# Loading V by whole heads (32 KB rows) in a one-token attention kernel that is bound by its loads

## The chip, the cores and the metric

The kernel runs on one core of one Trainium2 chip; no other core is used by it. The metric is the device time of one execution in microseconds (us). The kernel before takes 325.06 us, the median of four runs (324.63 to 325.5).

Engine names: PE is the matrix engine, DVE the vector engine, ACT the scalar engine, SP the engine whose sequencer issues the loads. "P·V" is the product of the softmax weights with V.

## The reference

```python
B, H, Sq, Sk, D = 1, 16, 1, 8192, 256      # q: one token; k and v: 64 MB each, bfloat16
def reference(q, k, v):
    scale = q.shape[-1] ** -0.5
    scores = jnp.einsum("bhqd,bhkd->bhqk", q, k) * scale
    p = _softmax(scores, axis=-1)
    return jnp.einsum("bhqk,bhkd->bhqd", p, v)
```

Every byte of K and V is read once, 134.2 MB in all. There are 16 heads, with 4 MB of K and 4 MB of V each.

## The kernel before

A head's K or V lies in SBUF (the core's on-chip memory) as 128 partitions by 64 columns of 256 numbers: partition p holds 64 neighbouring rows, 32 KB. The kernel loads *halves*: 32 of the 64 columns, 128 rows of 16 KB, 2 MB. There are four half-head buffers for K and four for V. Loads are issued by SP in one fixed order. A load into a buffer waits until that buffer's last reader is done, and holds up all loads behind it.

```python
LAST_CUT = (16, 8, 4, 4)      # columns per DMA: second half of V of the last head
BEFORE_CUT = (16, 16)         # first half of V of the last head
LAG = 4                       # V runs four halves (two heads) behind K
...
for n, kx in enumerate(kseq):             # kseq: (head, half) in order
    items.append(("k", *kx))
    while nv <= n - LAG:
        items.append(("v", *kseq[nv])); nv += 1
items += [("v", *kx) for kx in kseq[nv:]]
...
        if n >= slots:                    # the buffer's last readers
            waits = [f"{kind}free{n - slots}"] + ([f"ktfree{n - slots}"] if kind == "k" else [])
```

The scores of 24 of the 32 columns of each half are made by DVE (multiply and add up along the row, one instruction per column). The other 8 columns go to PE, which transposes them (`k_turn`) and multiplies (`k_score`). PE also makes P·V, one matmul of 256 output columns for each column of V. PE's program for head h, in order:

```python
softmax(h - 1)                 # transposes the maxima of head h-1
k_turn(2 * h)                  # first half of K of head h
softmax2(h - 1); k_score(2 * h); lmm(h - 1)
pv(2 * (h - 2))                # P·V, first half of head h-2
k_turn(2 * h + 1); k_score(2 * h + 1)
pv(2 * (h - 2) + 1)            # P·V, second half of head h-2
final(h - 2)
```

(`softmax`, `softmax2` and `lmm` are the small matmuls of the softmax: the maximum, its broadcast and the sum. `final` hands the finished head to ACT.) After the last head PE runs P·V of heads 14 and 15 with the small matmuls of the last softmax between them. PE takes its instructions strictly in this order, and each P·V matmul waits for the DMA that brings its column.

## Time and profile before

| | before |
|---|---|
| time, median | 325.06 us |
| span of the profiled execution | 322.9 us |
| first load packet starts, last load lands | 1.7 us, 319.6 us |
| V of head 13 fully landed | 299.9 us |
| last P·V matmul ends | 320.9 us |
| DVE busy, PE busy | 86%, 69% |

Here is the page of the kernel before, cut to three rows of its slices. The span is cut in 40 slices of 8.07 us. The PEclk row is PE's granted clock in tenths of full speed, the DMA row the busy share of the 16 DMA engines in tenths (9 is 90% or more), and GB/s what they moved.

```profile
PEclk9999999999698998989595989777989697897799
DMA  7999999999999999999999999999999999999993
GB/s 276 421 436 428 421 430 428 424 426 426 431 428 426 428 428 428 432 426 424 432 426 434 426 424 430 428 428 429 426 430 426 430 427 428 428 426 428 426 417 120
```

The DMA engines are full from the second slice to the last but one, at about 428 GB/s. This is a stream of loads, and everything else has to keep it full and to end soon after it. The Trainium skill ("DMA: Bandwidth & Descriptors", "Where 436 GB/s comes from") gives a ceiling of 435 GB/s for the SBUF ports. The trace agrees: it stands 1.6% below it. The same section says that for loads from HBM a lower figure binds, about 358 GB/s; that does not hold in this trace, where one core loads alone.

The end is the only part that is not stream. Here is PE's timeline of the kernel before at the end (start, length, engine, line, operation and number of instructions; in brackets the idle time before and what ended it):

```profile
299.91 8.81 PE L607 MATMUL acc<-Vb,E 128*1 128x256 bf16 x64 [1.33 <-DMA Vb<-in_v_dram]
308.56 0.38 PE L547 MATMUL misc<-ident,m 128*1 128x128 f32 x2
309.74 1.91 PE L607 MATMUL acc<-Vb,E 128*1 128x256 bf16 x16 [0.80 <-DMA Vb<-in_v_dram]
...
313.69 7.17 PE L607 MATMUL acc<-Vb,E 128*1 128x256 bf16 x64
```

At 299.91 us PE begins with the second half of V13, which has just landed; the first half is done already. At 309.74 it waits once more, for V14's second half. From there it has 96 columns left and never waits again: it is behind the stream, and it ends 1.2 us after the last landing.

The trace's load packets (one is one row of one load on one of the 16 engines) have these median times: 84 ns for 2 KB, 159 ns for 4 KB, 312 ns for 8 KB, 614 ns for 16 KB. So each costs about 75.5 ns per 2 KB and about 10 ns besides.

### The profile page before, as it was taken

The page shows a single profiled execution, that of the slowest core. Times are in us where ns is not written, and L with a number is a line of the kernel's source. Part 1 is how long each engine was busy: PE and PEld are TensorE (multiplying, and loading weights), DVE is VectorE, ACT ScalarE, POOL GpSimd, SP SyncE. Part 2 cuts the span into 40 slices and gives each one's busy share as a digit, 9 for nine tenths or more (in the row PEclk, how much of TensorE's full clock was granted, in tenths as well). Part 3 has the DMA queues.
Part 4 walks back from the last instruction along what each step waited for, and adds up shares of the span by engine and source line. Part 5 has one row for each costly group of instructions (what it writes and reads, how often), then busy time and mean ns, then how long its engine had stood idle before and what let it go on. Part 6 is the DMA issues. An engine that isn't in the chain of part 4 may idle for free.

```text
span 322.9 us, 6455 instructions
## 1 busy us (share of the span) xinstructions
PE 222.2 (69%) x2166; PEld 155.6 (48%) x2166; DVE 277.8 (86%) x1607; ACT 94.1 (29%) x185; POOL 0.2 (0%) x4
## 2 busy tenths in 40 slices
PE   1554328766586858686987756886665966668897
PEld 0333225655364635454564534564543644455565
DVE  3799999999999999999998988889988889888600
ACT  3362321432324242323142242212422123232010
POOL 0000000000000000000000000000000000000000
PEclk9999999999698998989595989777989697897799
DMA  7999999999999999999999999999999999999993
GB/s 276 421 436 428 421 430 428 424 426 426 431 428 426 428 428 428 432 426 424 432 426 434 426 424 430 428 428 429 426 430 426 430 427 428 428 426 428 426 417 120
DMA packets 10271, 134.37 MB, mean 416 GB/s; under 512 B 1154, under 2 KB 1171, under 8 KB 1940
## 3 DMA queue, kind: packets, MB, share of 16 engines
q1 hardware_dynamic: 10224, 134.22, 98.1%
q8 instruction: 5, 0.08, 0.1%
q14 instruction: 6, 0.05, 0.0%
q10 hardware_dynamic: 36, 0.02, 0.0%
HBM read 134.23 MB, written 0.01 MB: 416 GB/s over the span
## 4 chain that ended last, share of the span: by engine, by line
DVE 52%; DMA 37%; PE 5%; issue 5%; DVEq 1%; ACT 0%; SPq 0%
DVE prod L360 48%; DMA Kb<-in_k_dram 19%; DMA Vb<-in_v_dram 18%; PE acc L607 5%; DVE S L360 2%; DVE g L332 1%; DVE colf L286 0%; DVE recip L341 0%; DVEq L145 0%; DVE m L379 0%; ACT o L621 0%; DVEq L138 0%; DVEq L139 0%; SPq L319 0%; PE misc L558 0%
## 5 line engine op out<-in xcount | busy, mean ns | idle before, releaser
L360 DVE CUSTOM_DVE_ANT_0 prod<-Kb,qbc 128x256 bf16<-128x256 bf16 x768 | 269.1, 411 | 24.6 <-DMA Kb<-in_k_dram 15.7
L607 PE MATMUL acc<-Vb,E 128*1 128x256 bf16 x1024 | 147.4, 314 | 8.8 <-DMA Vb<-in_v_dram 8.8
L607 PEld LDWEIGHTS acc<-Vb,E 128*1 128x1 bf16 x1024 | 96.3, 96 | 52.4 <-DMA Vb<-in_v_dram 9.9
L502 ACT ACTIVATE KT<-tp 128x1024 bf16<-128x1024 bf16 x64 | 62.0, 1021 | 118.2 <-PE tp L493 118.2
L360 DVE DVE_READ_ACCUMULATOR2_ANT S<- 128x1 f32 x768 | 56.8, 74 | 0.0
L493 PE MATMUL tp<-identb,Kb 128*128 128x128 bf16 x512 | 38.2, 234 | 7.8 <-DMA Kb<-in_k_dram 7.8
L493 PEld LDWEIGHTS tp<-identb,Kb 128*128 128x128 bf16 x512 | 32.3, 105 | 15.7 <-issue 14.2
L519 PE MATMUL spe<-qcur,KT 128*128 128x1 bf16 x512 | 20.6, 165 | 19.7 <-ACT KT L502 19.7
L558 PE MATMUL misc<-g,ones_row 1*128 1x1 f32 x32 | 7.1, 287 | 36.1 <-DVE g L332 36.1
L519 PEld LDWEIGHTS spe<-qcur,KT 128*128 128x128 bf16 x512 | 16.4, 99 | 24.5 <-ACT KT L502 24.3
L621 ACT ACTIVATE o<-acc,recip 1x256 bf16<-1x256 f32 x16 | 7.4, 464 | 69.4 <-PE acc L607 69.4
L558 PEld LDWEIGHTS misc<-g,ones_row 1*128 1x128 f32 x32 | 5.7, 221 | 39.1 <-DVE g L332 38.8
L547 PE MATMUL misc<-ident,m 128*1 128x128 f32 x34 | 7.1, 293 | 18.6 <-DVE m L379 18.6
L547 PEld LDWEIGHTS misc<-ident,m 128*1 128x1 f32 x34 | 1.9, 82 | 22.0 <-DVE m L379 21.4
L565 ACT ACTIVATE negb<-misc 128x1 f32<-128x1 f32 x16 | 2.7, 171 | 27.4 <-PE misc L558 27.4
L332 DVE TENSOR_REDUCE g<-misc 1x1 f32<-1x128 f32 x17 | 4.7, 274 | 5.2 <-PE misc L547 5.2
L341 DVE RECIPROCAL recip<-misc 1x1 f32<-1x1 f32 x17 | 2.6, 151 | 4.6 <-PE misc L587 4.6
L572 ACT ACTIVATE E<-S,negb 128x64 bf16<-128x64 f32 x16 | 5.6, 348 | 0.7 <-ACT negb L565 0.2
L587 PE MATMUL misc<-ones_col,lsum 128*1 128x1 f32 x34 | 3.2, 164 | 3.7 <-ACT E L572 3.7
L439 ACT ACTIVATE qbc<-qb 128x256 bf16<-128x256 bf16 x14 | 5.6, 400 | 0.0
L532 ACT ACTIVATE S<-spe 128x16 f32<-128x16 f32 x16 | 2.9, 183 | 7.2 <-PE spe L519 7.2
L413 PE MATMUL tp<-q,identb 16*128 16x256 bf16 x15 | 4.1, 406 | 0.6 <-ACT qb L422 0.5
(29 smaller groups left out, 22.7 us busy)
## 6 DMA issues: line engine op xcount, KB each, us to landing
Kb<-in_k_dram SPq DMA_DIRECT2D x31, 2048.0 KB, 24.3
Vb<-in_v_dram SPq DMA_DIRECT2D x30, 2048.0 KB, 29.5
Vb<-in_v_dram SPq DMA_DIRECT2D x3, 1024.0 KB, 16.5
Kb<-in_k_dram SPq DMA_DIRECT2D x1, 1024.0 KB, 8.5
Kb<-in_k_dram SPq DMA_DIRECT2D x2, 256.0 KB, 3.0
Kb<-in_k_dram SPq DMA_DIRECT2D x1, 512.0 KB, 6.5
Vb<-in_v_dram SPq DMA_DIRECT2D x1, 512.0 KB, 12.7
Vb<-in_v_dram SPq DMA_DIRECT2D x2, 256.0 KB, 13.0
```

The source lines that it names most:

```text
L332: lambda e: e.tensor_reduce(g[0:1, s : s + 1], misc[s][0:1, MT0 : MT0 + P], AX.X, ALU.max),
L360: lambda e, slot=slot, c=c, col=col, h=h, r=(ttr - 1) % PROD: e.tensor_tensor_reduce(out=prod[:, r * D : (r + 1) * D], in0=Kb[slot][:, c * ...
L413: lambda e, i=i, src=src: e.matmul(bank[:, i * D : (i + 1) * D], lhsT=src[0], rhs=src[1], start=True, stop=True),
L439: lambda e: e.activation(out=qbc[:, s * D : (s + 1) * D], in_=qb[:, (h - 2) * D : (h - 1) * D], func=ACT.Copy),
L493: lambda e, c=c, hf=hf, i=(b * NH + hf) * P, view=view: e.transpose(view[:, i : i + P], Kb[slot][:, c * D + hf * P : c * D + (hf + 1) * P] ...
L502: lambda e, gn=gn, view=view: e.activation(out=KT[gn % KT_SLOTS][:, :], in_=view[:, 0 : GROUP * D], func=ACT.Copy),
L519: lambda e, b=b, hf=hf, oc=oc, gn=gn: e.matmul(spe[sl(h)][:, oc : oc + 1], lhsT=KT[gn % KT_SLOTS][:, (b * NH + hf) * P : (b * NH + hf + 1) ...
L547: lambda e: e.matmul(misc[s][0:1, MT0 : MT0 + P], lhsT=m[:, s : s + 1], rhs=ident[:, :], start=True, stop=True),
L558: lambda e: e.matmul(misc[s][:, BC0 : BC0 + 1], lhsT=ones_row[0:1, :], rhs=g[0:1, s : s + 1], start=True, stop=True),
L572: lambda e: e.activation(out=E[:, s * J : (s + 1) * J], in_=S[:, s * J : (s + 1) * J], func=ACT.Exp, bias=negb[:, h : h + 1], scale=SCALE, ...
L607: lambda e, c=c, col=col: e.matmul(a[0:1, 0:D], lhsT=E[:, col : col + 1], rhs=Vb[slot][:, c * D : (c + 1) * D], start=(x == 0 and c == 0), ...
L621: lambda e: e.activation(out=o[0:1, h * D : (h + 1) * D], in_=acc[s][0:1, 0:D], func=ACT.Copy, scale=recip[0:1, s : s + 1],),
```

## The change

The intent: a row of V becomes 32 KB instead of 16 KB, so that there are half as many rows with their fixed cost, and the last head's V comes in eight pieces so that PE can follow it closely.

- V has two buffers of a whole head, and heads 0 to 13 come in one 4 MB DMA each. K is still loaded in halves.
- A V buffer is freed by the whole head: the load of V of head h waits for both halves of P·V of head h-2.
- V follows one head behind K up to head 7 and two heads behind from head 8.
- P·V of both halves of head h-2 stands after the scores of head h.
- V14 comes in pieces of 32, 16 and 16 columns, V15 in 16, 8, 8, 8, 8, 8, 4 and 4.

```diff
-K_SLOTS = 2 * UNROLL
-V_SLOTS = 2 * UNROLL
...
-FIRST_CUT = (4, 4, 8, 16)
-LAST_CUT = (16, 8, 4, 4)
-BEFORE_CUT = (16, 16)
-LAG = 4
+K_CUTS = {0: (4, 4, 8, 16, 32)}
+V_CUTS = {14: (32, 16, 16), 15: (16, 8, 8, 8, 8, 8, 4, 4)}
+LAG_FROM = 8
...
+        for h in range(H):
+            loads.append(("k", h))
+            done = sum(kind == "v" for kind, _ in loads)
+            loads += [("v", x) for x in range(done, h + 1 - (1 if h < LAG_FROM else 2))]
+        loads += [("v", x) for x in range(sum(kind == "v" for kind, _ in loads), H)]
+
+        def cuts(kind, h):
+            return K_CUTS.get(h, (HALF, HALF)) if kind == "k" else V_CUTS.get(h, (J,))
...
                 if kind == "k":
...
+                    if h >= 2:
+                        waits = [f"kfree{2 * (h - 2) + i}", f"ktfree{2 * (h - 2) + i}"]
                 else:
...
+                    if h >= 2:
+                        waits = [f"vfree{2 * (h - 2)}", f"vfree{2 * (h - 2) + 1}"]
...
                 if h + 1 < H:
                     q_row(h + 1)
-                if h >= 2:
-                    pv(2 * (h - 2))
...
             if h >= 2:
+                pv(2 * (h - 2))
                 pv(2 * (h - 2) + 1)
                 final(h - 2)
```

More of the change, by code (lines that the diff above doesn't have):

```diff
@@ L178, in sem @@
             return ctx.enter_context(nc.semaphore(name))
-        Kb = [sb([P, HALF * D], dt, "Kb") for _ in range(K_SLOTS)]
-        Vb = [sb([P, HALF * D], dt, "Vb") for _ in range(V_SLOTS)]
+        Kb = [sb([P, J * D], dt, "Kb") for _ in range(2)]
+        Vb = [sb([P, J * D], dt, "Vb") for _ in range(2)]
         KT = [sb([P, GROUP * D], BF16, "KT") for _ in range(KT_SLOTS)]
@@ L213, in bass_standalone__mha_softmax__decode_kernel @@
         sems = {e: sem(f"s_{e}") for e in plan.ops}
-        s_k = [sem(f"s_k{i}") for i in range(K_SLOTS)]
-        s_v = [sem(f"s_v{i}") for i in range(V_SLOTS)]
-        s_first = [sem(f"s_f{i}") for i in range(len(FIRST_CUT) - 1)]
-        s_last = [sem(f"s_l{i}") for i in range(len(LAST_CUT) + len(BEFORE_CUT) - 2)]
+        s_k = [sem(f"s_k{i}") for i in range(4)]
+        s_v = [sem(f"s_v{i}") for i in range(2)]
+        s_piece = {}
         s_q = sem("s_q")
@@ L243, in bass_standalone__mha_softmax__decode_kernel, with pieces @@
         kseq = [(h, x) for h in range(H) for x in range(2)]
-        NIT = 2 * H
-        items, nv = [], 0
-        for n, kx in enumerate(kseq):
-            items.append(("k", *kx))
-            while nv <= n - LAG:
-                items.append(("v", *kseq[nv]))
-                nv += 1
-        items += [("v", *kx) for kx in kseq[nv:]]
-        n_of = {kx: n for n, kx in enumerate(kseq)}
-        def cuts(kind, n):
-            if kind == "k" and n == 0:
-                return FIRST_CUT
-            if kind == "v" and n == NIT - 1:
-                return LAST_CUT
-            if kind == "v" and n == NIT - 2:
-                return BEFORE_CUT
-            return (HALF,)
-        def landed(kind, n, c0, c1):
-            names, at = [], 0
-            if kind == "k" and n and n % K_SLOTS == 0:
-                names = [f"k{n}.0"] + [x for x in landed(kind, 0, c0, c1) if x != "k0.0"]
-                return names
-            for i, w in enumerate(cuts(kind, n)):
-                if at < c1 and at + w > c0:
-                    names.append(f"{kind}{n}.{i}")
-                at += w
-            return names
+        loads = []
+        for h in range(H):
[5 more added lines that the diff above has]
+            return K_CUTS.get(h, (HALF, HALF)) if kind == "k" else V_CUTS.get(h, (J,))
+        def landed(kind, n, c0, c1):
+            h, x = kseq[n]
+            def pieces(h):
+                at = 0
+                for i, w in enumerate(cuts(kind, h)):
+                    if at < x * HALF + c1 and at + w > x * HALF + c0:
+                        yield i
+                    at += w
+            if kind == "k" and h and h % 2 == 0:
+                return [f"k{h}.{x}"] + [f"k0.{i}" for i in pieces(0) if 0 < i < len(cuts(kind, 0)) - 1]
+            return [f"{kind}{h}.{i}" for i in pieces(h)]
         def dve(fn, name=None, waits=(), sem=None):
@@ L301, in bass_standalone__mha_softmax__decode_kernel @@
         plan.op("act", lambda e: e.dma_start(q16[:, :], q[0, :, 0, :]), "q", dma=(s_q, 16))
-        for kind, h, x in items:
-            n = n_of[(h, x)]
-            slots, sem_l, t, buf = (K_SLOTS, s_k, k, Kb) if kind == "k" else (V_SLOTS, s_v, v, Vb)
-            slot = n % slots
-            waits = []
-            if n >= slots:
-                waits = [f"{kind}free{n - slots}"] + ([f"ktfree{n - slots}"] if kind == "k" else [])
-            cs = cuts(kind, n)
+        for kind, h in loads:
+            t, buf = (k, Kb) if kind == "k" else (v, Vb)
+            cs = cuts(kind, h)
             at = 0
             for i, wd in enumerate(cs):
+                waits = []
+                last = i == len(cs) - 1
                 if kind == "k":
-                    s = sem_l[slot] if i == 0 else s_first[i - 1]
-                else:
-                    s = sem_l[slot] if i == len(cs) - 1 else s_last[i + (len(LAST_CUT) - 1) * (n == NIT - 2)]
+                    s = s_k[2 * (h % 2) + (i > 0)] if i == 0 or last else None
+                    if h >= 2:
+                        waits = [f"kfree{2 * (h - 2) + i}", f"ktfree{2 * (h - 2) + i}"]
+                else:
+                    s = s_v[h % 2] if last else None
+                    if h >= 2:
+                        waits = [f"vfree{2 * (h - 2)}", f"vfree{2 * (h - 2) + 1}"]
+                if s is None:
+                    s = s_piece[(kind, h, i)] = sem(f"s_{kind}{h}_{i}")
                 used[id(s)] = used.get(id(s), 0) + 16
@@ L318, in bass_standalone__mha_softmax__decode_kernel @@
                     "sp",
-                    lambda e, b=buf[slot], t=t, h=h, c=x * HALF, at=at, wd=wd: e.dma_start(
-                        b[:, at * D : (at + wd) * D], cols(t, h, c + at, c + at + wd)
+                    lambda e, b=buf[h % 2], t=t, h=h, at=at, wd=wd: e.dma_start(
+                        b[:, at * D : (at + wd) * D], cols(t, h, at, at + wd)
                     ),
-                    f"{kind}{n}.{i}",
+                    f"{kind}{h}.{i}",
                     waits,
@@ L349, in bass_standalone__mha_softmax__decode_kernel @@
         for n, (h, x) in enumerate(kseq):
-            slot = n % K_SLOTS
             if x == 0 and h % UNROLL == 0:
@@ L359, in bass_standalone__mha_softmax__decode_kernel @@
                 dve(
-                    lambda e, slot=slot, c=c, col=col, h=h, r=(ttr - 1) % PROD: e.tensor_tensor_reduce(
+                    lambda e, c=c, x=x, col=col, h=h, r=(ttr - 1) % PROD: e.tensor_tensor_reduce(
                         out=prod[:, r * D : (r + 1) * D],
-                        in0=Kb[slot][:, c * D : (c + 1) * D],
+                        in0=Kb[h % 2][:, (x * HALF + c) * D : (x * HALF + c + 1) * D],
                         in1=qbc[:, sl(h) * D : (sl(h) + 1) * D],
@@ L480, in k_turn @@
             h, x = kseq[n]
-            slot = n % K_SLOTS
             for gi in range(NG):
@@ L494, in k_turn @@
                                 view[:, i : i + P],
-                                Kb[slot][:, c * D + hf * P : c * D + (hf + 1) * P],
+                                Kb[h % 2][:, (x * HALF + c) * D + hf * P : (x * HALF + c) * D + (hf + 1) * P],
                                 identb[:, :],
@@ L600, in pv @@
             h, x = kseq[n]
-            slot = n % V_SLOTS
             a = acc[sl(h)]
@@ L609, in pv @@
                         lhsT=E[:, col : col + 1],
-                        rhs=Vb[slot][:, c * D : (c + 1) * D],
+                        rhs=Vb[h % 2][:, (x * HALF + c) * D : (x * HALF + c + 1) * D],
                         start=(x == 0 and c == 0),
```

## The prediction

> **What bounds it now.** The 16 DMA engines. The page's slices and the stage table give a DMA share of 1.00 and 427 to 428 GB/s from 12 to 300 us; the packets leave no gap between 1.7 us and the last landing at 319.7 us. DVE is busy 86%, PE 69%; landings come 24 to 30 us after the issue, so the queue never runs dry. Only the end is not DMA: the timeline shows PE waiting at 309.7 us for the second half of V14, then running 96 P·V matmuls without a DMA wait to 320.9 us, 1.2 us after the last V piece landed.
>
> **What the change does.**
>
> 1. *Longer packets.* In the trace's packets a 16 KB row takes 614 ns, 8 KB 312, 4 KB 159, 2 KB 84: about 75.5 ns per 2 KB plus 10 ns each. So a 32 KB row should take about 1,218 ns against 2 x 614. 14 heads x 8 rows per engine x 10 ns is -1.1 us; fewer completion writes (9 ns each) -0.1; finer last pieces +0.2. Net -1.1 us, all on the path. The Trainium skill ("DMA: Bandwidth & Descriptors", "Where 436 GB/s comes from") puts the ceiling at 435 GB/s; this trace is at 428, so longer rows of V alone cannot give 1%.
>
> 2. *Coarser landings.* P·V of a head waits for all of V (4 MB, 9.8 us of stream), and PE does both halves in one run. Matmuls in P·V start 109 ns apart at full clock, 213 ns at half. In the steady state this is off the path. I reckon 20 us or more of slack for slots in the late phase, 4 us in the early one; DVE waits about 2 us more per head for the maximum (PE is in P·V), inside its slack (17.3 us busy per 19.6 us head). Tightest is V2: its slot frees after P·V of head 0, near 63 us (begin 53.5, 64 matmuls, some 20 cold); the stream needs it near 64. Expected loss 0.3 us, at worst 2 to 3.
>
> 3. *The tail.* V13 now lands whole, about 20 us before the end, and PE has 192 matmuls left instead of 160 or fewer: 192 x 109 ns = 20.9 us, 0.9 us for the small softmax matmuls, and 1.7 to 3 us of half clock, because PE idles about 7 us before V13 lands. (The Trainium skill, "TensorE: Matmul & The Clock Gate", Part 1, says that an idle window of about 3.4 us brings the half clock; the trace shows such stretches, one at 300.8 us.) So PE ends about 3.9 us after the last landing, against 1.2: +2.7 us. The eight pieces help only a PE that waits; here it lags.
>
> Sum: -1.1 + 0.3 + 2.7 = about +1.6 us: **326.6 us**, 8 in 10 between 323.2 and 329.2. Faster by over 2%: 2%; within 2%: 95%; slower by over 2%: 3%.
>
> **What would show it.** Packets of 32,768 bytes near 1,218 ns; last landing about 1 us earlier (318.6); DMA share still 1.00, save perhaps a small dip near 64 us; P·V of V13, V14 and V15 as one unbroken PE run from about 299 us to 322.5 us, with no wait for the eight pieces; a half-clock stretch at its start; no new DVE-for-K waits.
>
> **What would make it wrong.** A PE that catches up with V15's pieces: then the tail ends 0.6 us after the last landing, the result near 323 us. Long rows split by the hardware: no gain in 1. V2 or V3 issued late: a gap in the stream.

## The result, and the profile after

| | before | after |
|---|---|---|
| time, median (range) | 325.06 us (324.63 to 325.5) | 329.27 us (329.14 to 329.35) |
| ratio | | 1.0129 (1.0111 to 1.0147) |
| span of the profiled execution | 322.9 us | 327.5 us |
| V13 fully landed | 299.9 us | 300.8 us |
| last load landed | 319.6 us | 323.5 us |
| last P·V matmul ends | 320.9 us | 325.4 us |

The change makes the kernel 1.3% slower. A ratio here is the mean time of one kernel's fast runs over the mean of the other's in the same rounds, so it isn't quite the ratio of the medians. The bracket is a 95% interval.

The same three rows of the page, after (slices of 8.19 us):

```profile
PEclk9999999969679695976959795875959578595799
DMA  7999999899999999999999999999999999999694
GB/s 255 430 446 422 419 448 410 316 448 404 438 427 454 404 430 446 416 440 420 424 450 418 426 462 396 436 422 430 436 428 460 397 432 452 404 432 430 278 356 160
```

Two holes have come into the stream: one in the eighth slice (316 GB/s) and one in the third slice from the end (278 GB/s). PE's clock is at half more often. The stage view places the holes. Its columns are the stretch in us, its length, the busy time with the number of instructions of PE, of PE's weight loads, of DVE, ACT and POOL, then PE's clock, the DMA share and GB/s. First the kernel before, in the stretches of the two holes:

```profile
61.80:64.40 2.60, 2.29 (x28) 1.66 (x26) 2.56 (x16) 1.19 (x2) 0.00 (x0) 1.00 1.06 441
64.40:67.00 2.60, 0.86 (x18) 0.76 (x18) 2.60 (x16) 1.63 (x4) 0.00 (x0) 1.00 0.99 422
308.40:312.00 3.60, 2.80 (x25) 1.84 (x23) 0.28 (x1) 0.00 (x1) 0.00 (x0) 1.00 1.02 423
```

The same stretches of the changed kernel:

```profile
61.80:64.40 2.60, 2.38 (x28) 1.57 (x25) 2.57 (x17) 1.09 (x2) 0.00 (x0) 1.00 0.77 233
64.40:67.00 2.60, 0.55 (x12) 0.54 (x13) 2.60 (x16) 1.45 (x3) 0.00 (x0) 1.00 0.71 290
308.40:312.00 3.60, 3.60 (x35) 2.77 (x34) 0.00 (x0) 0.47 (x1) 0.00 (x0) 1.00 0.23 52
```

The share, the second number from the end, falls from about 1 to 0.77 and 0.71 in the early hole, which is 2.6 x 0.23 + 2.6 x 0.29 = 1.4 us of the whole stream, and to 0.23 in the late one, which is 2.8 us. This view counts a packet whole where it starts. With packets cut at the window's edges, the trace has the engines idle for 1.6 us between 60 and 66 us, and for 3.2 us in the late window. The 16 rows that start the stream again after the early hole also took 1.87 us each in the mean, 0.65 us more than the usual 1.22. So the early hole is about 2.3 us of stream in this run.

What the early hole waits for is seen in the loads that SP issues (the timeline of SP's queue, after), with PE's timeline before it:

```profile
53.84 0.37 PE L510 MATMUL spe<-qcur,KT 128*128 128x1 bf16 x8 [0.54 <-ACT KT L493]
54.14 8.71 PE L597 MATMUL acc<-Vb,E 128*1 128x256 bf16 x64
```

```profile
36.30 8.70 SPq L312 DMA_DIRECT2D Kb<-in_k_dram  x2
62.88 0.33 SPq L312 DMA_DIRECT2D Vb<-in_v_dram  x1
63.26 1.45 SPq L312 DMA_DIRECT2D Kb<-in_k_dram  x2
```

V2 needs V0's buffer. P·V of head 0, 64 matmuls, runs from 54.14 to 62.85 us, and V2 is issued at 62.88. K of head 3, the last load ahead of it, was issued by 45.0 us, and its second half completes on the first of the 16 engines at 61.80 us and on the last at 64.88 us. So most engines ran dry. In the kernel before, the same stretch of SP's queue has K of head 4 ahead of V2, and V2's first half, which needs only the first half of V0's buffer, goes out at 56.38 us:

```profile
44.72 0.43 SPq L319 DMA_DIRECT2D Vb<-in_v_dram  x1
53.85 0.33 SPq L319 DMA_DIRECT2D Kb<-in_k_dram  x1
56.38 0.33 SPq L319 DMA_DIRECT2D Vb<-in_v_dram  x1
```

PE's timeline at the end, after:

```profile
296.91 0.37 PE L510 MATMUL spe<-qcur,KT 128*128 128x1 bf16 x8 [0.56 <-ACT KT L493]
300.92 13.37 PE L597 MATMUL acc<-Vb,E 128*1 128x256 bf16 x96 [3.63 <-DMA Vb<-in_v_dram]
314.12 0.38 PE L538 MATMUL misc<-ident,m 128*1 128x128 f32 x2
...
318.29 7.15 PE L597 MATMUL acc<-Vb,E 128*1 128x256 bf16 x64
```

PE now stands idle for 3.6 us until the whole of V13 is there, and has 192 columns left instead of 160. From 300.92 us to 325.43 us, 24.5 us, it waits for no load again: the eight pieces of V15 are there when it comes to them. The first 96 matmuls take 13.37 us. In the trace 25 of the 192 stand 213 ns apart, and nearly all others 109 ns: PE's clock is at half from 296.3 to 306.5 us. In the kernel before, the stretch from V13's landing to PE's end was 320.9 - 299.9 = 21.0 us.

So the change of the span of 4.6 us has two visible parts: PE begins on the V that it waited for 1.0 us later (300.92 against 299.91), and needs 3.6 us more from there (24.5 against 20.9). By the spacing of the matmuls these 3.6 us are 32 more of them at 109 ns (3.5 us) and ten more at half clock (25 against 15 in the kernel before, 1.0 us), less about 1.0 us that the kernel before waits for V14.

The packets: a 32 KB row takes 1,215 ns (median), a 16 KB row 613 ns, so 11 ns are saved per pair of rows.

### The profile page after: what moved, and what is told of

It is laid out like the page before. It is cut to its first block, busy times and chain, and to the rows that moved or that the text cites. A ratio compares the mean times of both kernels' runs of the same rounds, so it can differ in the third digit from the quotient of the medians.

```text
span 327.5 us, 6434 instructions
## 1 busy us (share of the span) xinstructions
PE 225.7 (69%) x2166; PEld 163.0 (50%) x2166; DVE 277.6 (85%) x1607; ACT 93.6 (29%) x185; POOL 0.2 (0%) x4
## 4 chain that ended last, share of the span: by engine, by line
DMA 45%; DVE 24%; PE 23%; issue 4%; ACT 3%; SPq 0%; DVEq 0%
DMA Vb<-in_v_dram 27%; DVE prod L352 22%; PE acc L597 21%; DMA Kb<-in_k_dram 18%; ACT KT L493 2%; PE tp L484 1%; DVE S L352 1%; PE misc L549 1%; DVE g L325 0%; ACT E L563 0%; SPq L312 0%; DVE colf L276 0%; PE spe L510 0%; PE misc L578 0%; ACT negb L556 0%
## 5 line engine op out<-in xcount | busy, mean ns | idle before, releaser
L597 PE MATMUL acc<-Vb,E 128*1 128x256 bf16 x1024 | 142.5, 311 | 19.2 <-DMA Vb<-in_v_dram 19.2
L352 DVE DVE_READ_ACCUMULATOR2_ANT S<- 128x1 f32 x768 | 55.7, 73 | 0.0
L484 PE MATMUL tp<-identb,Kb 128*128 128x128 bf16 x512 | 44.7, 257 | 11.6 <-DMA Kb<-in_k_dram 11.6
L484 PEld LDWEIGHTS tp<-identb,Kb 128*128 128x128 bf16 x512 | 38.2, 117 | 17.0 <-issue 13.1
L510 PE MATMUL spe<-qcur,KT 128*128 128x1 bf16 x512 | 21.8, 167 | 19.8 <-ACT KT L493 19.8
L510 PEld LDWEIGHTS spe<-qcur,KT 128*128 128x128 bf16 x512 | 17.4, 103 | 26.0 <-ACT KT L493 25.9
L549 PE MATMUL misc<-g,ones_row 1*128 1x1 f32 x32 | 7.4, 297 | 24.8 <-DVE g L325 24.8
L414 ACT ACTIVATE qb<-tp 128x512 bf16<-128x512 f32 x7 | 3.9, 595 | 3.3 <-PE tp L405 3.3
```

Source lines behind the costliest of these rows:

```text
L352: lambda e, c=c, x=x, col=col, h=h, r=(ttr - 1) % PROD: e.tensor_tensor_reduce(out=prod[:, r * D : (r + 1) * D], in0=Kb[h % 2][:, (x * HAL ...
L414: lambda e: e.activation(out=qbc[:, a * D : b * D] if first else qb[:, (a - 2) * D : (b - 2) * D], in_=bank[:, 0 : (b - a) * D], func=ACT. ...
L484: lambda e, c=c, hf=hf, i=(b * NH + hf) * P, view=view: e.transpose(view[:, i : i + P], Kb[h % 2][:, (x * HALF + c) * D + hf * P : (x * HA ...
L510: lambda e, b=b, hf=hf, oc=oc, gn=gn: e.matmul(spe[sl(h)][:, oc : oc + 1], lhsT=KT[gn % KT_SLOTS][:, (b * NH + hf) * P : (b * NH + hf + 1) ...
L549: lambda e: e.matmul(misc[s][:, BC0 : BC0 + 1], lhsT=ones_row[0:1, :], rhs=g[0:1, s : s + 1], start=True, stop=True),
L597: lambda e, c=c, col=col: e.matmul(a[0:1, 0:D], lhsT=E[:, col : col + 1], rhs=Vb[h % 2][:, (x * HALF + c) * D : (x * HALF + c + 1) * D], s ...
```

## The experiments

The theory after the result (A): the longer rows give about 1.1 us. The early hole takes that back and more, because V2's buffer comes free by the whole head. At the end PE gets V13 too late and too cold, and the late hole costs nothing, because PE is behind the stream there. Each experiment changes the changed kernel, called "after" below. Each was timed against the kernel before in its own rounds; the median of the kernel before there was 324.92 us for e1 to e4 and 324.88 us for the others. All gave correct results.

### e1: V15 in a buffer of its own

Rival: the hole of 2.8 us at 308 us is what costs. V15 needs V13's buffer, and P·V of head 13 ends at 310.8 us. The K buffer of head 14 is free by then, so V15 goes there and nothing else changes.

```diff
+                    if h == H - 1:
+                        waits = [f"{w}{x}" for x in (2 * H - 4, 2 * H - 3) for w in ("kfree", "ktfree")]
-                    if h >= 2:
+                    elif h >= 2:
                         waits = [f"vfree{2 * (h - 2)}", f"vfree{2 * (h - 2) + 1}"]
...
-                        rhs=Vb[h % 2][:, ...],
+                        rhs=(Kb[0] if h == H - 1 else Vb[h % 2])[:, ...],
```

(The destination of the load is changed likewise, and V15's last piece has a semaphore of its own.)

> V of head 15 goes into K's buffer 0, which is free by then, so that its load no longer waits for P.V of head 13. Theory A (the end is bound by PE: 192 matmuls from the landing of V13 on, without a wait): the stream's gap at 308.4 to 312.0 us disappears, the last landing comes 3 us or more earlier, yet the P.V run still starts near 300.9 us and ends near 325.4 us: time 329.3 us, within 0.4. Rival G (the gap in the stream, 3.2 us of 16 engines, costs time): 326 us.

Measured: 329.36 us (328.63 to 329.58), ratio 1.0129 (1.0112 to 1.0145), the same as after. The hole is gone in the stage view of e1:

```profile
308.40:312.00 3.60, 3.60 (x35) 2.77 (x33) 0.00 (x0) 0.46 (x1) 0.00 (x0) 1.00 1.00 412
```

The last load lands 320.9 us into the span instead of 323.5. Yet the chain that ended last (start, length, what) is after's:

```profile
300.91 0.14 issue
301.04 13.44 PE acc L599 x96
...
318.62 7.02 PE acc L599 x64
```

So a hole of 2.8 us in the stream, 15 us before the end, costs nothing: PE is the limit there. The rival falls.

### e2: V13 in two halves; e8: its control

PE's loop over heads is a rolled loop whose bodies have to wait for the same things, so heads 14 and 15 are taken out of it and written out.

```diff
-V_CUTS = {14: (32, 16, 16), 15: (16, 8, 8, 8, 8, 8, 4, 4)}
+V_CUTS = {13: (32, 32), 14: (32, 16, 16), 15: (16, 8, 8, 8, 8, 8, 4, 4)}
...
-        plan.mark("pe")          # end of PE's loop: now in front of head 14
```

> V of head 13 lands in two halves; the last two heads of PE's loop are unrolled for it (a rolled body may not differ). Theory A: P.V of head 13 starts near 297.3 us instead of 300.9, the slot of V15 frees near 307 us so that the gap at 308 us goes too, and PE ends 3.3 to 4.6 us earlier, bound by PE or by the last landing: time 324.7 to 326.0 us. A theory in which the end is bound by the eight pieces of V15 themselves (small transfers): no gain, 329 us.

> Control: the changed kernel with the last two heads of PE's loop unrolled and nothing else, as e2, e5 and e7 needed it. Theory A and every rival: 329.3 us, within 0.4.

Measured: e8, the unrolling alone, 329.19 us, ratio 1.0126 (1.0111 to 1.0141): no effect. e2: 325.98 us (325.8 to 327.11), ratio 1.0040 (1.0017 to 1.0064), 3.3 us under after. PE's timeline of e2:

```profile
298.20 12.02 PE L597 MATMUL acc<-Vb,E 128*1 128x256 bf16 x96
...
314.21 4.53 PE L597 MATMUL acc<-Vb,E 128*1 128x256 bf16 x40
318.99 1.03 PE L597 MATMUL acc<-Vb,E 128*1 128x256 bf16 x8 [0.25 <-DMA Vb<-in_v_dram]
320.26 1.91 PE L597 MATMUL acc<-Vb,E 128*1 128x256 bf16 x16 [0.23 <-DMA Vb<-in_v_dram]
```

PE begins 2.7 us earlier, right after the scores of head 15 and with no wait, and now does wait for the last pieces of V15, 0.2 us at a time. One of the 14 whole-head DMAs, cut in two, gives back most of the loss. The late hole is gone too, because V13's buffer is freed earlier.

### e7: the clock of PE at V13's landing

How much of the end is the half clock? Forty-two matmuls without use keep PE occupied while it waits for V13. They multiply the identity's first column with a row of q into columns of a PSUM bank that nothing reads.

```diff
             k_turn(2 * h)
+            if h == H - 1:
+                warm(10)
...
             k_turn(2 * h + 1)
+            if h == H - 1:
+                warm(10)
             k_score(2 * h + 1)
+            if h == H - 1:
+                warm(22)
```

> The changed kernel with 42 matmuls without use (into a free part of a PSUM bank) in PE's program for head 15, ahead of P.V of head 13, and the last two heads of PE's loop unrolled for them. Theory A (28 of the 192 matmuls of the final run are at half clock, 3.0 us, because PE was little used before V13 landed): the half-clock stretch from 296 to 306 us shrinks or goes, the run of 24.5 us falls to 21.5 to 22.5 us, time 326.3 to 327.5 us. Rival (the slow matmuls come from V's data just landing, or the end is bound by something else): 329.3 us.

Measured: 326.58 us (326.29 to 327.3), ratio 1.0047 (1.0033 to 1.0062), 2.6 us under its control e8. In e7's timeline the first 96 matmuls of the end take 10.64 us instead of 13.37:

```profile
298.51 2.56 PE L625 MATMUL acc<-qb,identb 128*1 128x256 bf16 x22
301.65 10.64 PE L597 MATMUL acc<-Vb,E 128*1 128x256 bf16 x96 [0.58 <-DMA Vb<-in_v_dram]
```

Not one of the 192 matmuls is slow any more; the run from 301.65 us to 323.45 us takes 21.8 us. The Trainium skill ("TensorE: Matmul & The Clock Gate", Part 1) says that the clock drops after an idle window of about 3.4 us and comes back after about 3.4 us of sustained activity. The traces agree in part. In after the clock is at half for 10.2 us, three times 3.4, and comes back at the end of 3.4 us in which PE was busy throughout (303.1 to 306.5 us). But it drops at 296.3 us without an idle window: in the 3.4 us before, PE was busy for 2.0 us with transposes and small matmuls. Work without use in such gaps was enough to keep the clock up here.

How much the half clock costs is known only roughly. The medians of e8 and e7 say 2.6 us, with about 0.7 us from the intervals of the two ratios. But e8's own profiled run has 13 slow matmuls at the end (1.4 us) where after has 25 (2.6 us), and the profiled runs of e8 and e7 differ by 1.8 us: the cold stretch differs from run to run. The gains of e2 and e7 are not to be added: both are ways for PE to be less behind.

### e3: the order of the loads that removes the early hole

If V lags two heads from head 3 on, K4 goes ahead of V2.

```diff
-LAG_FROM = 8
+LAG_FROM = 3
```

> V lags two heads behind K from head 3 on instead of from head 8: K of head 4 goes ahead of V of head 2, which is the load that came late. Theory A (gap of 1.6 us at 61.9 to 64.4 us, with 0.6 us of slow packets at the restart, all of it on the path): gap gone, P.V of head 13 starts 2.2 us earlier, time 327.1 us (326.7 to 327.6). Rival: the gap is made good later by slack, 329.3 us.

Measured: 327.21 us (326.71 to 327.53), ratio 1.0065 (1.0048 to 1.0082), 2.1 us under after. V2 is issued as late as in after, at 63.25 us, but the stage view of e3 shows no hole:

```profile
61.80:64.40 2.60, 2.60 (x31) 1.93 (x29) 2.56 (x16) 0.84 (x2) 0.00 (x0) 1.00 1.00 416
64.40:67.00 2.60, 0.90 (x19) 0.76 (x18) 2.60 (x18) 2.05 (x5) 0.00 (x0) 1.00 0.96 410
```

So the early hole is on the path and isn't made good later. Its size is less sharp than its existence. The medians say 2.1 us, with an interval of each ratio of about 0.17%, or 0.6 us. In the profiled runs that keep after's order of loads there (after, e1, e2, e4, e7, e8), the engines' idle time in this hole is between 1.4 and 2.6 us. In the profiled runs of after and e3, P·V of V13 begins 1.3 us earlier in e3 (299.58 against 300.92 us), and PE's final run, whose cold part differs from run to run, is 0.5 us shorter.

### e4: PE's old order

The other candidate for the late V2 is that the change moved the first half of P·V behind the second half of K.

```diff
                 if h + 1 < H:
                     q_row(h + 1)
+                if h >= 2:
+                    pv(2 * (h - 2))
...
             if h >= 2:
-                pv(2 * (h - 2))
                 pv(2 * (h - 2) + 1)
```

> Only PE's order is put back: P.V of the first half of head h-2 stands again before the transposes of the second half of K of head h. Theory A (V2 is late because the slot is freed by whole heads, and the work of PE before that is the same in either order): V2 is still issued at 62.5 to 63 us, the gap at 62 us stays within 0.3 us; at the end PE stands before V13 with K15's second half not transposed, so the run after V13's landing grows by about 3 us: time 332 us (331 to 333). Rival M (the moved P.V made V2 late): gap gone, 2.2 us saved there.

Measured: 331.23 us (330.45 to 332.02), ratio 1.0200 (1.0174 to 1.0226), 2.0 us over after. V2 is issued at 62.90 us, as in after (62.88), so the moved P·V isn't the cause. What is left is the pair that the change brought in: V2 waits for the whole of V0's buffer, and it stands next in the queue, ahead of K4. e3 shows that the order alone removes the hole, with the buffer still freed by the whole head. Freeing it by halves in after's order was not tried. At the end PE waits for V13 with half of K15 still in front of it:

```profile
300.68 4.93 PE L597 MATMUL acc<-Vb,E 128*1 128x256 bf16 x32 [3.34 <-DMA Vb<-in_v_dram]
305.54 1.07 PE L484 MATMUL tp<-identb,Kb 128*128 128x128 bf16 x16
```

The expected 3 us were 2 us; the first half of P·V took 4.93 us here, with less of it at half clock. Given whole heads of V, moving P·V was right.

### e5 and e6: both mends, and the worth of the long rows

e5 puts the edits of e2 and e3 together. e6 is e5's order with V of heads 0 to 13 in halves, so 16 KB rows, the buffer still freed by the whole head.

```diff
# e5
+V_CUTS = {13: (32, 32), 14: (32, 16, 16), 15: (16, 8, 8, 8, 8, 8, 4, 4)}
+LAG_FROM = 3
# e6
+V_CUTS = {h: (32, 32) for h in range(14)} | {14: (32, 16, 16), 15: (16, 8, 8, 8, 8, 8, 4, 4)}
+LAG_FROM = 3
```

> Both mends at once: V lags two heads behind K from head 3 on, and V of head 13 lands in halves. Theory A (the early gap, about 2.1 us, and PE's late start on V13, about 3.3 us, are separate terms that add, with the longer V rows as the gain that is left): 329.3 - 2.1 - 3.3 = 323.9 us (323.2 to 324.6), 1.1 us under the kernel before, with P.V at the end waiting for the last pieces of V15. If the two overlap: 325 to 326 us.

> As e5, but V of heads 0 to 13 comes in two DMAs of half a head each (16 KB rows, as in the kernel before), the slot still freed by whole heads. Theory A (a 32 KB row takes 1,215 ns against 2 x 613): 104 rows per engine of V0 to V12 cost 11 to 13 ns more each, 1.1 to 1.4 us, and PE still waits for the last pieces: 1.2 us slower than e5, about the kernel before, 325.1 us. Rival (row length is worth nothing, e5 gains by order alone): the same time as e5 within 0.3 us.

Measured: e5 323.65 us (323.42 to 324.84), ratio 0.9972 (0.9956 to 0.9988): it is the fastest version here and beats the kernel before by 0.3%, by its interval a real if small gain. Two of its six runs were at 324.8 us, the others near 323.5; why isn't known. e6: 324.99 us (324.25 to 325.9), ratio 0.9997, the time of the kernel before. The end of e5 follows the stream (PE's timeline of e5):

```profile
294.67 13.11 PE L597 MATMUL acc<-Vb,E 128*1 128x256 bf16 x96
...
311.78 4.62 PE L597 MATMUL acc<-Vb,E 128*1 128x256 bf16 x40
316.63 1.03 PE L597 MATMUL acc<-Vb,E 128*1 128x256 bf16 x8 [0.23 <-DMA Vb<-in_v_dram]
317.86 1.91 PE L597 MATMUL acc<-Vb,E 128*1 128x256 bf16 x16 [0.19 <-DMA Vb<-in_v_dram]
```

The two mends add: 2.1 + 3.3 = 5.4 us expected from e3 and e2, and 329.27 - 323.65 = 5.6 us measured (5.1 us by the ratios). The long rows are worth 1.3 us by the medians of e6 and e5 and 0.8 us by their ratios, whose intervals leave about 0.6 us either way. The packet times give 1.1 us (104 rows per engine x 11 ns).

### e9: V15 in five pieces instead of eight

```diff
-V_CUTS = {13: (32, 32), 14: (32, 16, 16), 15: (16, 8, 8, 8, 8, 8, 4, 4)}     # e5
+V_CUTS = {13: (32, 32), 14: (32, 16, 16), 15: (32, 16, 8, 4, 4)}
```

> As e5, with V of head 15 in five pieces (32, 16, 8, 4, 4 columns, sizes of the kernel before) instead of eight. Theory A (in e5 PE reaches V15 at 311.8 us and follows its pieces; a first piece of 32 columns would land only near 313.6): the stream gets about 0.4 us shorter by fewer small packets, PE starts on V15 up to 1.8 us later and ends 0 to 0.8 us later: 323.6 to 324.5 us. If the number of pieces matters only through its packets: 323.2 us.

Measured: 325.29 us (324.59 to 327.03), ratio 1.0013 (0.9991 to 1.0034). By the ratios that is 0.4%, or 1.3 us, over e5, and more than expected. PE's timeline of e9:

```profile
313.02 0.19 PE L578 MATMUL misc<-ones_col,lsum 128*1 128x1 f32 x2
314.67 7.15 PE L597 MATMUL acc<-Vb,E 128*1 128x256 bf16 x64 [1.46 <-DMA Vb<-in_v_dram]
```

PE waits 1.46 us for the first 32 columns, and then all 64 matmuls follow without a break, so the wait is carried to the end in full. So the eight pieces, for none of which PE waits while it is behind (after), pay once it isn't. e9 ran on another chip than e5; each was compared with the kernel before on its own chip.

### e10: K of the odd heads by whole heads as well

```diff
-K_CUTS = {0: (4, 4, 8, 16, 32)}                                              # e5
+K_CUTS = {0: (4, 4, 8, 16, 32)} | {h: (64,) for h in range(1, 16, 2)}
```

(The one DMA waits for both halves of the buffer.)

> As e5, and K of the odd heads too in whole heads (32 KB rows). Theory A (the path is the stream; DVE has the slack to start an odd head 4.9 us later): 64 rows per engine x 11 to 13 ns = 0.7 to 0.8 us faster than e5, 322.9 us. Rival (DVE, busy 86%, falls behind, or K15's late landing delays the last softmax): 324 us or more, with new waits of DVE for K or of PE for DVE at the end.

Measured: 327.16 us (325.97 to 329.19), ratio 1.0072 (1.0047 to 1.0098): slower than e5 by 3.5 us in the median, so theory A's number was wrong and the rival's bound held, for one of its reasons and a new one. (e10, like e9, ran on another chip than e5.) The new one is a hole, in the stage view of e10:

```profile
80.50:83.50 3.00, 3.00 (x35) 2.27 (x34) 2.34 (x14) 0.59 (x2) 0.00 (x0) 1.00 0.62 202
```

K5 waits for both halves of K3's buffer and is issued at 82.09 us, too late, as V2 was. The other is that PE starts P·V of head 13 at 298.93 us, against 294.67 in e5: K15 lands whole, DVE waits 5.2 us for it, until 290.58 us, and its scores come late. In all DVE waits 18.3 us for K, against 6.1 in e5. How the 3.5 us divide between the two was not tried.

## Why the prediction was right or wrong

The prediction was 326.6 us, slower by 1.6 us; measured were 329.27 us, slower by 4.2 us and just outside the range (323.2 to 329.2). Direction and mechanism were right; two terms of the sum were too small.

- **Longer packets, -1.1 us: right.** A 32 KB row was put at 1,218 ns and took 1,215. e6 against e5 measures 0.8 to 1.3 us.
- **Early hole, +0.3 us: the main failure.** The place (V2) and its issue time (about 63 us; measured 62.88) were right. The step that failed is "the stream needs it near 64". That is near when the slowest of the 16 engines finishes what is queued. A DMA's landing is the last of 16 completions: the second half of K3 completes from 61.80 to 64.88 us, so the first engine ran dry 3.1 us before that landing, and on average they stood idle for 1.6 us. V2's first packet came 1.0 us after its issue (63.84 us), too. e3 measures the cost: 2.1 us by medians; the trace shows 2.3 us, idle engines and the slow first rows together. The prediction named this as its risk ("at worst 2 to 3") but counted 0.3.
- **The tail, +2.7 us: right mechanism, too small, and one hole overlooked.** P·V of V13, V14 and V15 is one unbroken run, with half clock at its start, as forecast. The run was put at 23.5 to 24.8 us by its terms, of which 1.7 to 3 us half clock, with about 3.9 us after the last landing. It took 24.5 us, against 20.9 us before, so 3.6 us more than before where 2.7 were forecast for the end. Its half clock is 2.6 us in this trace (25 matmuls), within the forecast; but the forecast end of 322.5 us uses the low end of the run. The start was forecast near 299 us, and the early hole made it 300.9.
- **"20 us or more of slack for slots in the late phase": wrong.** It leaves out that no K stands between V13, V14 and V15 at the end, so V15 waits for P·V of head 13: the second hole, 2.8 us. The last landing was then 323.5 us instead of 318.6. e1 shows that this mistake cost the forecast nothing, which was luck: PE was behind the stream there anyway.
- **No new waits of DVE for K: right.** They came to 15.0 us in total, against 15.7 before.
- **"The eight pieces help only a PE that waits; here it lags": right** for this kernel (no wait for them in after), and e9 shows the other side.

The sum as measured: -1.1 (rows) + about 2.1 (early hole) + 3.6 (PE's end) is 4.6 us, as in the span, for 4.2 us in the medians. The middle term is known to about 0.8 us.

## What to carry to other kernels

In a kernel that is bound by its loads, a larger DMA saves its rows' fixed cost, here about 0.3%, and makes three things coarser: when the consumer can start, when a buffer comes free, and how much work is left when the last data is there. Keep large DMAs for the middle. Where the stream is short of queued loads, put another load ahead of the one that has to wait (e3), and cut the DMAs in the last heads (e2). Before you trust a stream to stay full, count from the first of the 16 engines that finishes, not from the landing. And a hole in the stream costs time only where the stream is what ends last.

## What the Trainium skill lacked or had wrong

- "DMA: Bandwidth & Descriptors" (rules for kernel authors) advises at least 1 MiB per DMA for bandwidth. It doesn't say what row length does above that: from 16 KB to 32 KB rows, with DMAs of 2 to 4 MB, the pair of rows fell from 1,226 to 1,215 ns, 0.9%.
- The same page says ("Why a DMA increments its semaphore by 16 and not by 1") that the engines finish independently. It has no size for this: in a full stream the 16 completions of one 2 MB load were spread over 3.1 us (61.80 to 64.88 us), and over 1.6 us in the loads after the hole (103.85 to 105.45 us).
- "TensorE: Matmul & The Clock Gate" (Part 1) calls the warm-up penalty under 1% of a typical kernel. Here one cold start in the last 25 us cost 1.4 us (e8's slow matmuls) to 2.6 us (e7 against e8), 0.4 to 0.8% of the kernel. That is within the page's figure, but all of it lay on the path. The page asks for matmuls ahead of a benchmark, but doesn't mention matmuls without use as a way to keep the clock up; e7 shows that 42 of them were enough.
